# Three edits to the warm-up of a routed mixture-of-experts kernel: later weight steps, one shared tile for the first two units, and a different turn order

## The chip, the cores and the metric

The kernel runs on one core of one Trainium2 chip. The metric is the device time of one launch in microseconds (us); lower is better. The time before is 1173.4 us, the median of three runs that lie between 1171.6 and 1175.38 us.

## What is computed

The input x has 8 sequences of 2880 tokens with 192 features. Each of 8 heads (24 features) is replaced by a causal 7-tap weighted sum along the sequence. The 23040 resulting tokens then pass a two-level router (4 groups of 4 experts), and each token goes through the one expert that it picked. Cut to what matters:

```
x_unf = x_pad[:, idx, :].reshape(B, S, K, H, group)          # 7 neighbours of each token
x = einsum('hk,bskhg->bshg', softmax(weight), x_unf)         # 8 heads, K = 7
g_idx = argmax(x @ w_group); e_idx = argmax(x @ w_expert[g]) # one group, one expert in it
for each of the 16 experts (192 -> 1024 -> 192):
    out[tokens of e] = g_w * e_w * (relu(x[tokens] @ w1[e]) @ w2[e])
```

## The kernel before, in words

The work has two kinds. A **unit** is a stretch of 4, 8 or 12 blocks of 120 tokens; there are 18 of them, of 4, 8, 12, 8, 8 and 8 blocks and then twelve of 12. A unit loads its rows of x into the tile `xin` (L205, L207), runs the 7-tap sum as eight TensorE products with a band matrix (L409), one for each head, copies each into the tile `xc` on ScalarE (L418), transposes `xc` (L428, L438), forms the router's logits (L448, L451), picks group and expert on VectorE (L483 to L512), writes `xc` with the router's weight to a table of tokens in HBM, `xcd` (L514, issued on ScalarE's queue), counts positions with two small products (L523, L524), builds a list of token numbers for each expert with one-hot products (L549 to L570) and scatters it to `idtab` (L581, on GpSimd). In the text below the units are called the first to the eighteenth; in the code they are `u` = 0 to 17.

A **slot** is up to 256 tokens of one expert. It reads its token numbers (`idp`, L976), gathers the rows from `xcd` (L653), transposes them (L666, L667) and runs the two layers (L684; L702, L706). All fp32 products of a slot are built from pairs of rounded and residual parts, so an expert's weights are loaded in five transfers (L602, L603, L604, and L606 twice; 1.84 MB with the part that is loaded twice) and then **split** in four steps: a copy on ScalarE (L618, L626, L633) and a subtraction on VectorE (L619, L627, L634) each. The raw weights have three buffers of each of their two kinds (`raw` and `rawc`), and a buffer comes free when its split is done.

The slots come in three portions. The first holds one slot of each of the 16 experts and can open when the first five units have been scattered (`NEED = 5`). The second needs twelve units, the third all eighteen.

Units are Python generators. One call of `step()` in the program advances one live unit to its next `yield`. Up to three units are live in the warm-up; a new one joins when the youngest has taken a given number of steps (`SK`). Before the change the live units take turns in a circle. The warm-up loop counts its steps in `k`, and the list `KPRE` says after which step the loads of the first expert are issued, then its four splits, then the loads of the second expert and three of its splits. When the fifth unit's list has been scattered, the loop ends; the first two slots are opened, 100 more steps are taken (`AHEAD`), and the first slot is transposed. From there the steps of the remaining units are spread between the parts of the slots.

This is the order of the program. The order on each engine is laid out afterwards by a planner, which lets an instruction pass others that its own model of the time sees as not ready. A few instructions are pinned among each other (`pin`): the transfers of x up to the fifth unit, the first expert's five transfers, and ScalarE's copies of the splits. On one engine, and on one issuing queue, what stands behind a waiting instruction waits too.

The tile `xin` has two buffers; the first two units (4 and 8 blocks) share one. The tile `xc` has three, and before the change each unit takes one, so that the fourth unit has to wait until the first unit's write to `xcd` has landed, the fifth for the second's, the sixth for the third's.

Of the kernel before, what the change touches and what calls it, by code (L numbers as in the profile page):

```python
# [9 lines left out]
F32 = mybir.dt.float32  # L10
# [10 lines left out]
P = 128  # L21
BT = 120
UB = 12
# [13 lines left out]
def conv_moe_kernel(  # L37
# [50 lines left out]
    units = []  # L88
# [7 lines left out]
    NEED = 5  # L96
# [37 lines left out]
    FRH = 0  # L134
    UG = [0, 5, 6, 1, 5, 8, 0, 5, 6, 0, 5, 7, 0, 5, 6, 2, 5, 10]
    SK = [8, 8, 6, 11, 10, 9, 9]
    KPRE = [5, 6, 16, 33, 35, 47, 63, 68, 79]
    CEU = 0
    CEH = (1, 3, 5, 7)
    PF = 1  # L140
# [18 lines left out]
    pa2 = ctx.enter_context(tc.tile_pool(name="pa2", bufs=XCB))  # L159
# [13 lines left out]
    XE = XW + D2  # L173
# [72 lines left out]
    def clear_table():  # L246
        pin(PINC1, nc.sync.dma_start(
            out=bass.AP(idtab.tensor, idtab.offset, [[CAP, E], [LR, LF], [1, LR]]), in_=fill[0:LF * E, 0:LR],
        ))
        pin(PINC2, nc.sync.dma_start(  # L250
            out=idtab[DUMMY:DUMMY + SLOT, :].rearrange("(p r) c -> p (r c)", p=8), in_=fill[0:8, 0:SLOT // 8],
        ))
# [102 lines left out]
    for t in xg:  # L355
        nc.gpsimd.memset(t, 0.0)

    bands = {}

    def gaps(u):  # L360
# [3 lines left out]
    def unit(u, pre=None):  # L364
# [14 lines left out]
            if u < PFL:  # L379
                load_unit(v)  # L380
        yield
        xc = pa2.tile([P, UB, XE], F32, name="xc", bufs=3)
        split = u >= FRU
        if split:
            if "h" not in bands:
# [526 lines left out]
    credit = [0.0]  # L912
    live = []
    done = [0]
    routed = [0, 0]
    needs = {need: pi for pi, (need, _) in enumerate(portions)}

    def step():

        if routed[0] < NU and len(live) < lead[1] and (not live or max(live, key=lambda a: a[0])[1] >= (lead[0] or SK[min(routed[0], len(SK)) - 1])):  # L920
            u = routed[0]
            live.append([u, 0, unit(u, xin0 if u == 0 else None)])
            routed[0] += 1
        if not live:
            return
        done[0] += 1
        cur = live.pop(0)
        cur[1] += 1
        try:
            next(cur[2])  # L930
            live.append(cur)
        except StopIteration:
            pass
# [11 lines left out]
    def advance(rate):  # L945
        credit[0] += rate
        while credit[0] >= 1.0:
            credit[0] -= 1.0
            step()
# [84 lines left out]
    def open_slot(i):  # L1034
        if i >= len(plan):
            return
        pi, e, s = plan[i]
        if closing:
            wait[0] -= 1
            if wait[0] <= 0 or closing[0] == pi:  # L1040
                open_portion(closing.pop())
        while pi != "tail" and pi not in idps:
            step()
            if closing:
                open_portion(closing.pop())
        rate[0] = max(
            [(stages_to(portions[q][0]) - done[0]) / (max(starts[q] - MARGIN - i, 1) * 2 * NF)
             for q in starts if q not in idps] + [0.0])
        if late and (pi == "tail" or e >= 2):
            next(late[0], None)  # L1050
        if pi == "tail":
            W = tail_weights(i)
            ids = idps["tail"][:, e]
            known = N
        else:
            W = pre.pop(e if pi == 0 else None, None) or weights(e * D, e * F, PENG(pi, e)) if s == 0 else opened[i - 1][0]
            ids = idps[pi][:, e, 2 * s:2 * s + 2]
            known = sum(n for _, n in units[:portions[pi][0]]) * BT
        for q in range(i + 1, i + 1 + TAHEAD):
            if tab[0] is not None and len(units) == routed[1]:  # L1060
                tail_weights(q, False)
        opened[i] = (W, ids)
        gathered[i] = gather(ids, known, tiles(i))
# [3 lines left out]
    while routed[1] < portions[0][0]:  # L1067
        step()
        if k == KW:
            router_weights()  # L1070
        if k == 4:
            clear_table()
        for i in [i for i, kk in enumerate(KPRE) if kk == k]:
            e, q = divmod(i, 5)
            if q == 0 and e < 2:
                pre[e] = weights(e * D, e * F, {k: nc.gpsimd for k in PREG[e]})
            elif e < 2 and 4 * e + q <= KN:
                split_one(pre[e])
        k += 1
# [157 lines left out]
```

## Time and profile before

| | before |
|---|---|
| median of three runs | 1173.4 us (1171.6 to 1175.38) |
| the profiled execution | 1170.84 us, its span 1169.0 us |
| TensorE busy | 1111.7 us, 95% |
| VectorE, ScalarE, GpSimd busy | 804.5, 690.1, 498.2 us |
| mean granted TensorE clock | 0.977 |
| transfers | 195.63 MB, 167 GB/s over the span |

PE is TensorE, PEld its loading of the stationary operand, DVE VectorE, ACT ScalarE, POOL GpSimd, SP the engine that issues most transfers; a q behind a name is that engine's issuing queue. In a row of the timeline the columns are start, duration in us, engine, line, operation, output and inputs, shape and count, and in brackets how long the engine had been idle and what released it. In the view of stretches the columns are the stretch, its length, each engine's busy time with its number of instructions, the granted TensorE clock as a fraction, the DMA engines' busy share and GB/s. In the view of waits a row says who waited for whom, with the total in us, the number of times and the longest.

### The profile page before, as it was taken

To read this page: it belongs to the slowest core of one execution; us is meant where nothing else is said; L and a number is where in the kernel's file an instruction comes from. 1 tells how busy PE (TensorE), PEld (TensorE's weight loads), DVE (VectorE), ACT (ScalarE), POOL (GpSimd) and SP (SyncE) were. 2 spreads that over 40 slices of the span, in tenths; PEclk is the share of its full clock that TensorE was granted. 3 is DMA by queue.
4 is the path that set the end of the run, shared out by engine and by line. 5 is a ranking of instruction groups with operands and counts; after the bars stand their busy time and mean duration, and the time that the engine had idled before them with its cause. 6 is when DMAs were issued, how large, how long until landed. Compare 5 with 4: busy or idle time off the path is not lost.

```text
span 1169.0 us, 23803 instructions
## 1 busy us (share of the span) xinstructions
PE 1111.7 (95%) x8468; PEld 1079.3 (92%) x8468; DVE 804.5 (69%) x1668; ACT 690.1 (59%) x1374; POOL 498.2 (43%) x443
## 2 busy tenths in 40 slices
PE   5887999999999999999999999999999999999994
PEld 4766999998999999999999999999999999998984
DVE  4756788887877676666678565656565656688772
ACT  5544677657655555656554555555555656677772
POOL 2103234434434343434344444444444445578771
PEclk8879999999999999999999999999999999999997
DMA  8766699989775654546354574545454545599960
GB/s 228 217 182 178 173 213 230 226 203 268 217 194 143 165 156 118 143 116 170 95 162 95 155 203 128 142 128 141 130 141 128 140 118 167 146 243 266 248 160 19
DMA packets 167212, 195.63 MB, mean 167 GB/s; under 512 B 22500, under 2 KB 144333, under 8 KB 167086
## 3 DMA queue, kind: packets, MB, share of 16 engines
q1 hardware_dynamic: 125006, 140.41, 44.6%
q0 software_dynamic: 18752, 35.85, 10.5%
q10 hardware_dynamic: 23328, 17.80, 6.2%
q8 instruction: 67, 1.10, 0.4%
q14 instruction: 59, 0.48, 0.1%
HBM read 158.79 MB, written 36.58 MB: 167 GB/s over the span
## 4 chain that ended last, share of the span: by engine, by line
PE 79%; DVE 5%; DMA 4%; issue 3%; ACT 3%; another core or an unknown queue 0%; POOL 0%; POOLq 0%; ACTq 0%; DVEq 0%; SPq 0%
PE ph L684 33%; PE po L702 21%; PE po L706 10%; PE pm L409 3%; DMA xg<-xcd,idpt 3%; PE pm L451 2%; PE pm L666 2%; PE pm L667 2%; PE pm L428 1%; PE ph L719 1%; PE pm L448 1%; DVE hl L690 1%; DVE ohl L549 1%; DMA idtab<-lsi,rowi 1%; ACT cw L633 1%
## 5 line engine op out<-in xcount | busy, mean ns | idle before, releaser
L702 PE MATMUL po<-cw,hh 128*128 128x384 f32 x1424 | 443.4, 369 | 5.9 <-DVE ys L754 5.9
L684 PE MATMUL ph<-xa,ah 128*128 128x256 f32 x1424 | 390.2, 296 | 1.9 <-DVE xa L669 1.5
L757 POOL DMA_INDIRECT out<-ys,idp x160 | 167.8, 1049 | 447.4 <-DVE ys L754 348.8
L706 PE MATMUL po<-cw,hl 128*128 128x192 f32 x1424 | 357.3, 251 | 0.0
L690 DVE SCALAR_TENSOR_TENSOR hl<-ph,hh 128x512 fp32r<-128x512 f32 x356 | 241.2, 686 | 163.5 <-ACT hh L689 149.3
L689 ACT ACTIVATE hh<-ph 128x512 fp32r<-128x512 f32 x356 | 210.8, 594 | 205.8 <-PE ph L684 170.2
L702 PEld LDWEIGHTS po<-cw,hh 128*128 128x128 f32 x1424 | 268.6, 189 | 9.7 <-DVE ys L754 7.6
L684 PEld LDWEIGHTS ph<-xa,ah 128*128 128x128 f32 x1424 | 271.0, 190 | 5.0 <-DVE xa L669 1.6
L706 PEld LDWEIGHTS po<-cw,hl 128*128 128x128 f32 x1424 | 272.6, 191 | 1.5
L653 POOL DMA_INDIRECT xg<-xcd,idp x160 | 190.0, 1187 | 62.0 <-issue 29.6
L684 PE MATMUL ph<-xb,bh 128*128 128x256 f32 x712 | 201.9, 284 | 0.3 <-DVE xb L673 0.3
L684 PE MATMUL ph<-xb,bl 128*128 128x256 f32 x712 | 201.8, 283 | 0.0
L684 PE MATMUL ph<-xa,al 128*128 128x256 f32 x712 | 201.3, 283 | 0.0
L684 PEld LDWEIGHTS ph<-xa,al 128*128 128x128 f32 x712 | 136.5, 192 | 2.1
L684 PEld LDWEIGHTS ph<-xb,bl 128*128 128x128 f32 x712 | 136.7, 192 | 0.0
L684 PEld LDWEIGHTS ph<-xb,bh 128*128 128x128 f32 x712 | 136.2, 191 | 0.4 <-DVE xb L673 0.4
L634 DVE TENSOR_TENSOR cw<-rawc,cw 128x768 fp32r<-128x768 f32 x114 | 105.3, 953 | 18.3 <-ACT cw L633 13.7
L619 DVE TENSOR_TENSOR al<-raw,ah 128x1024 fp32r<-128x1024 f32 x57 | 70.5, 1238 | 38.8 <-ACT ah L618 21.6
L754 DVE SCALAR_TENSOR_TENSOR ys<-po,xg,ys 128x192 f32<-128x192 f32 x187 | 76.2, 416 | 23.2 <-ACT ys L753 18.1
L633 ACT ACTIVATE cw<-rawc 128x768 fp32r<-128x768 f32 x114 | 91.0, 837 | 1.8 <-DMA rawc<-in_moe_w 1.4
L672 ACT ACTIVATE xb<-pm 64x256 fp32r<-64x256 f32 x98 | 36.0, 367 | 93.4 <-DVE xa L669 86.2
L753 ACT ACTIVATE ys<-po,xg 128x192 f32<-128x192 f32 x187 | 75.8, 418 | 22.2 <-PE po L706 12.0
(216 smaller groups left out, 1561.0 us busy)
## 6 DMA issues: line engine op xcount, KB each, us to landing
rawc<-in_moe_w SPq DMA_DIRECT2D x114, 384.0 KB
raw<-in_moe_w SPq DMA_DIRECT2D x57, 512.0 KB
raw<-in_moe_w SPq DMA_DIRECT2D x114, 256.0 KB
xcd<-xc ACTq DMA_DIRECT2D x13, 1085.6 KB
xin<-in_x SPq DMA_DIRECT2D x7, 1134.0 KB
xc<-in_moe_w SPq DMA_DIRECT2D x18, 384.0 KB
xin<-in_x SPq DMA_DIRECT2D x6, 1039.5 KB
xin<-in_moe_w SPq DMA_DIRECT2D x9, 512.0 KB
```

The costliest lines, as they stand in the source:

```text
L619: eng.get(k, nc.vector).tensor_tensor(out=al, in0=ra, in1=ah.bitcast(F32), op=ALU.subtract)
L633: pin(PINW, nc.scalar.activation(out=cw[:, fs, 0, :], in_=rc[k - 2], func=AF.Copy))
L634: eng.get(k, nc.vector).tensor_tensor(out=cw[:, fs, 1, :], in0=rc[k - 2], in1=cw[:, fs, 0, :].bitcast(F32), op=ALU.subtract,)
L653: nc.gpsimd.indirect_dma_start(out=xs[:, t, :], out_offset=None, in_=xcd[0:known, :], in_offset=bass.IndirectOffsetOnAxis(ap=ids[:, t, 0:1 ...
L684: nc.tensor.matmul(out=hp[:, j], lhsT=wgt[:, fs], rhs=xx, start=i == 0, stop=i == len(ops) - 1)
L689: nc.scalar.activation(out=hh, in_=hp, func=AF.Relu)
L690: nc.vector.scalar_tensor_tensor(out=hl, in0=hp, scalar=0.0, in1=hh.bitcast(F32), op0=ALU.max, op1=ALU.subtract,)
L702: nc.tensor.matmul(out=oo[t][:, 0:2 * D], lhsT=hh[:, j, ts], rhs=cw[:, f].rearrange("p a d -> p (a d)"), start=f == 0, stop=False,)
L706: nc.tensor.matmul(out=oo[t][:, 0:D], lhsT=hl[:, j, ts], rhs=cw[:, f, 0, :], start=False, stop=f == NF - 1,)
L753: nc.scalar.activation(out=ys[:, t, :], in_=oo[t][:, D:2 * D], func=AF.Copy, scale=g)
L754: nc.vector.scalar_tensor_tensor(out=ys[:, t, :], in0=oo[t][:, 0:D], scalar=g, in1=ys[:, t, :], op0=ALU.mult, op1=ALU.add,)
L757: nc.gpsimd.indirect_dma_start(out=outviews[nscat[0] % len(outviews)], out_offset=bass.IndirectOffsetOnAxis(ap=ids[:, t, 0:1].bitcast(U32) ...
```

## The change

It has three parts. The list `KPRE` gets other step numbers: the first expert's loads go from step 5 to step 10 and its splits from 6, 16, 33 and 35 to 26, 29, 36 and 39; the second expert's loads go from 47 to 88 and three of its splits from 63, 68 and 79 to 128, 134 and 144. The second unit no longer takes an `xc` tile of its own: it uses blocks 4 to 11 of the first unit's. And `step()` no longer takes the live units strictly in a circle: once exactly one of the first five units is live beside later ones, that unit gets every second step and the others share the rest.

```
-    KPRE = [5, 6, 16, 33, 35, 47, 63, 68, 79]
+    KPRE = [10, 26, 29, 36, 39, 88, 128, 134, 144]
...
+    shared = []
...
-        xc = pa2.tile([P, UB, XE], F32, name="xc", bufs=3)
+        if u == 1:
+            xc = shared[0][:, units[0][1]:UB]
+        else:
+            xc = pa2.tile([P, UB, XE], F32, name="xc", bufs=3)
+            if u == 0:
+                shared.append(xc)
...
+    odd = [False]
...
-        cur = live.pop(0)
+        first = [a for a in live if a[0] < NEED]
+        others = [a for a in live if a[0] >= NEED]
+        cur = live[0]
+        if len(first) == 1 and others:
+            odd[0] = not odd[0]
+            cur = first[0] if odd[0] else others[0]
+        live.remove(cur)
```

## The prediction

> **What bounds the kernel now.** I read the page first (busy shares), then the stretches, then TensorE's waits, then the timeline of the first 120 us.
>
> ```profile
> span 1169.0 us, 23803 instructions
> PE 1111.7 (95%) x8468; PEld 1079.3 (92%) x8468; DVE 804.5 (69%) x1668; ACT 690.1 (59%) x1374; POOL 498.2 (43%) x443
> ```
>
> TensorE is busy 95% of the span. The change leaves its work as it is, so it can only take away, or add, time in which TensorE idles or runs at a reduced clock. The stretches say where that time is:
>
> ```profile
> 0.00:20.60 20.60, 10.74 (x56) 9.88 (x56) 9.45 (x51) 11.44 (x34) 8.38 (x32) 1.00 0.80 206
> 20.60:30.00 9.40, 6.17 (x18) 4.41 (x18) 4.56 (x14) 5.10 (x11) 0.00 (x0) 0.64 1.04 281
> 30.00:46.40 16.40, 16.40 (x141) 15.54 (x140) 11.00 (x42) 13.00 (x36) 2.09 (x1) 1.00 0.83 238
> 46.40:64.00 17.60, 8.74 (x57) 7.13 (x57) 13.53 (x54) 4.87 (x16) 1.95 (x2) 0.61 0.72 175
> 64.00:80.00 16.00, 14.88 (x79) 12.82 (x78) 7.50 (x33) 7.47 (x22) 0.97 (x1) 0.68 0.70 206
> ...
> 101.50:120.00 18.50, 11.78 (x69) 9.76 (x69) 10.04 (x41) 6.33 (x18) 6.00 (x6) 0.82 0.65 169
> ...
> 400.00:1100.00 700.00, 695.60 (x5346) 686.43 (x5345) 472.81 (x855) 413.02 (x770) 329.52 (x285) 1.00 0.55 153
> ```
>
> From 400 to 1100 us there is nothing to gain: 695.6 of 700 us are busy at full clock. In the warm-up there is. I count a stretch's loss as its idle time plus busy time times (1 - clock). From 20.6 to 30: 3.23 + 6.17 x 0.36 = 5.4 us. From 46.4 to 64: 8.86 + 8.74 x 0.39 = 12.3. From 64 to 80: 1.12 + 14.88 x 0.32 = 5.9. From 101.5 to 120: 6.72 + 11.78 x 0.18 = 8.8. From 30 to 46.4 nothing is lost. What TensorE waited for, and what ScalarE waited for behind it:
>
> ```profile
> PE ph L409 <- DVE band L339: 8.7, 1, 8.7
> PE pm L570 <- DVE ohv L557: 4.6, 4, 1.6
> PE pm L409 <- ACT lg L454: 3.5, 1, 3.5
> PE ph L570 <- DVE ohv L557: 3.4, 1, 3.4
> PE ph L409 <- DMA xin<-in_x: 3.2, 1, 3.2
> PE pm L409 <- ACT xc L418: 2.2, 1, 2.2
> ```
>
> ```profile
> ACT xc L418 <- DMA xcd<-xc: 12.0, 3, 6.0
> ACT lg L454 <- remote: 3.9, 1, 3.9
> ```
>
> The 8.7 us for the band matrix at the start is not touched.
>
> **Part one: the first expert's loads behind the third unit's x.** Counting the generators' steps in the code, the second unit's first step, which also requests the third unit's x, is step 9. The loads at step 5 stand ahead of it, at step 10 behind it; both are pinned, so the queue follows.
>
> ```profile
> 12.84 0.35 SPq L207 DMA_DIRECT2D xin<-in_x  x1
> 23.84 1.31 PE L409 MATMUL ph<-xin,band 126*120 126x288 f32 x2 [3.23 <-DMA xin<-in_x]
> 24.95 1.17 PE L409 MATMUL pm<-xin,band 126*120 126x288 f32 x2
> ...
> 86.71 0.65 PE L409 MATMUL po<-xin,band 126*120 126x288 f32 x2
> 87.20 0.65 PE L409 MATMUL pm<-xin,band 126*120 126x288 f32 x2
> ```
>
> TensorE is through with the second unit at 20.6 and waits 3.23 us for an x that was issued at 12.84 behind the expert. With the expert's 1.84 MB out of its way, x comes 1.84 MB / 281 GB/s = 6.5 us earlier, at about 17.3, before it is wanted. After the wait a pair of products takes 1.17 us, later 0.65 (and starts 0.49 apart): the clock is reduced for a while, and that goes with the wait. So up to 5.4 us. In return the first expert's data come 12 x 126 rows x 768 B = 1.16 MB, or 4.1 us, later; its copies are moved 10 to 20 steps back as well, so that they should rarely hold up ScalarE. I take a gain of 5.0; the ends are 0 (ScalarE stuck behind a late copy for as long as TensorE was behind x) and 5.4.
>
> The Trainium skill ("TensorE: Matmul & The Clock Gate", Part 1) says that the array gets half its pulses until it has been busy for some 3.4 us, so that every wait costs 1.7 us more. The trace agrees here (2.2 us of clock lost from 20.6 to 30). With this wait and two later ones gone, that rule's clock term would be 5.1 us in place of the 4.2 that I use (2.2 here, 2.0 below); the sum by it would be -12.4 in place of -11.5, an estimate.
>
> **Part two: the second expert's splits late.** Steps 63, 68 and 79 lie among the fourth unit's heads; 128, 134 and 144 lie after the fifth unit's, before its list (step 154 after the change).
>
> ```profile
> 35.73 1.23 DVE L619 TENSOR_TENSOR al<-raw,ah 128x1024 fp32r<-128x1024 f32 x1 [0.80 <-ACT ah L618]
> 39.34 1.05 ACT L626 ACTIVATE bh<-raw 128x1024 fp32r<-128x1024 f32 x1
> 40.42 1.22 DVE L627 TENSOR_TENSOR bl<-raw,bh 128x1024 fp32r<-128x1024 f32 x1 [1.39 <-ACT bh L626]
> 40.96 5.06 SPq L606 DMA_DIRECT2D rawc<-in_moe_w  x2
> 43.11 0.33 ACTq L514 DMA_DIRECT2D xcd<-xc  x1
> 51.40 0.34 ACT L418 ACTIVATE xc<-ph 120x192 f32<-120x192 f32 x1 [5.26 <-DMA xcd<-xc]
> 55.18 0.32 ACTq L514 DMA_DIRECT2D xcd<-xc  x1
> 62.58 0.33 ACT L418 ACTIVATE xc<-pm 120x192 f32<-120x192 f32 x1 [6.03 <-DMA xcd<-xc]
> ```
>
> The stall from 46.4 on is a chain. The second unit's write is issued at 43.11 and lands 8.29 us later; the fifth unit's first copy needs its buffer, so ScalarE stands still for 5.26 us; behind it stands the third unit's exponential, so the third unit's write goes out only at 55.18, and 7.4 us later the sixth unit's copy has waited 6.03. Ahead of 43.11 stand 1.23 + 1.22 us of the second expert's subtractions on VectorE and a 1.05 us copy on ScalarE. Without them I put the write 2.4 us earlier. Its landing shortens too: the loads that share the transfers then (40.96) are the third expert's, which need buffers that the second expert's splits set free. By size the third unit's landing bounds it, 7.4 x 8/12 = 4.9 us; between that and 8.29 I take 6. So 4.7 of the 5.26 us go, and of the 6.03 some 2.4.
>
> In TensorE's time: the 2.2 us wait goes, one ohv wait of 1.6 goes with VectorE's relief, 1.6 of the 3.4 and 0.6 of a last one of 1.6 go: 6.0 us. Of the 8.2 us lost to the clock from 46.4 to 80 (3.4 + 4.8) I take 2.0, less than their share. Together 8.0; the ends are 0 and 18.2.
>
> The cost is at the new place.
>
> ```profile
> 34.66 1.05 ACT L618 ACTIVATE ah<-raw 128x1024 fp32r<-128x1024 f32 x1
> 42.71 0.84 ACT L633 ACTIVATE cw<-rawc 128x768 fp32r<-128x768 f32 x1
> 44.66 0.95 DVE L634 TENSOR_TENSOR cw<-rawc,cw 128x768 fp32r<-128x768 f32 x1
> 85.15 0.97 POOL L581 DMA_INDIRECT idtab<-lsi,rowi  x1 [12.81 <-DVE lsi L578]
> 91.43 0.39 SPq L976 DMA_DIRECT2D idp<-idtab  x1
> 96.33 1.07 POOL L653 DMA_INDIRECT xg<-xcd,idp  x1 [10.21 <-DMA idp<-idtab]
> 109.50 0.27 PE L666 MATMUL pm<-ident,xg 128*128 128x128 f32 x1
> ```
>
> It is 1.05 + 1.05 + 0.84 = 2.9 us of ScalarE and 1.23 + 1.22 + 0.95 = 3.4 us of VectorE, in a stretch where each is busy 7.5 of 16 us. What queues behind them is the fifth unit's choice of expert and its write. Ends 0 and 3.4; I take 1.5, since both engines are half idle. The loads of the second expert are not pinned: the third expert's (40.96) already run some 190 steps ahead of their place, so they may stay early. That costs nothing while the raw buffers hold, and is no gain.
>
> **Part three: the shared tile.** It spares the fourth unit's wait on the first unit's write: 12.0 - 5.26 - 6.03 = 0.7 us on ScalarE, while TensorE was fully busy (30 to 46.4). The fifth unit still needs the second unit's write. I take 0; ends 0 and -0.7.
>
> **Part four: the turns.** The warm-up loop falls from 162 to 155 steps. Five of the seventh unit's heads, 5 x 0.49 = 2.4 us of TensorE, move behind the fifth unit's list. The work is moved, not removed, and 100 steps still follow before the first slot. I take 0; ends -2.4 and 2.4. The chain from list to first transpose (85.15 to 109.50, 24.35 us) stays covered by sixth to ninth unit as before; the 8.8 us lost from 101.5 on, 3.5 of them behind a ScalarE wait whose source the profile does not name, I leave, with ends of 4 us either way. The main part is replanned too, without a reason for either sign: 0, ends 2.
>
> **The sum.** -5.0 - 8.0 + 1.5 = -11.5 us. The profiled execution took 1170.84 us (span 1169.0 and 1.84 around it), so 1159.3; the median of the runs shown stands 2.56 higher, so 1161.9.
>
> **The rivals.**
> - *The waits on the writes stay* (the buffers are asked for in the same order, and the copies come earlier by as much as the writes do). Only part one is left: -5.0 + 1.5, so 1169.9. For it: the sixth unit's wait of 6.03 us follows a landing of 7.4 us that nothing shortens directly. Against: the relief on VectorE lies ahead of the writes alone.
> - *Slower: the third expert's loads fall into the opening chain.* They wait for the second expert's splits. If those run at 78 us or later, 1.84 MB (6.5 us at 281 GB/s) lies beside the fifth unit's write, the list's scatter, the read of `idp` and the first gathers, which TensorE must wait out. 6.5 + 3.4 - 5.0 = +4.9, so 1178.3. It decides from the point where the third expert's L606 issues lie between the fifth unit's write and the first gather. Against: step 128 lies among the sixth unit's first heads, one of whose copies ran at 62.58, and from 101.5 on the engines have bandwidth free (0.65). The Trainium skill ("DMA: Bandwidth & Descriptors", Queues, rings and completion order) says that an engine takes turns between the queues that have work; by that such loads would halve a write's rate, which speaks for this rival.
> - *More*: the whole chain from 46.4 to 80 dissolves: -5.0 - 18.2 + 1.5, so 1151.7. For it: each wait there causes the next, and the clock falls with them.
> - *The change does not do what it says*: the planner already reorders, and puts x or the splits where they were. 1173.4.
>
> **How the numbers follow.** The forecast gets 0.40 (1156 to 1168 by itself), the waits that stay 0.15, slower 0.20, more 0.13, nothing 0.12. 0.3% (3.5 us) is about what a measurement of this kernel can tell from no change. Faster by more: 0.40 + 0.13 + half of 0.15 = 0.61. Within: the other half and 0.09 of the 0.12, 0.16. Slower: 0.20 + 0.03 = 0.23. The range from 1149 to 1178 reaches from the far case to the slower one, with the unknown ends of the opening in it.
>
> **What would show it.** Part one: the L207 issue of the third unit ahead of the first L602 behind the table's clearing, no wait of L409 on x near 20 us, clock near 1 from 20 to 30. Part two: no second split before the fifth unit's heads, the total of ScalarE's waits on xcd down from 12.0 to some 5. Its cost: waits of VectorE's L483 chain on copies of the splits. The turns: the scatter of the fifth unit some 12 us ahead of 85.15 and the first L684 ahead of 110.9 by as much. I am wrong if the first L684 is earlier by that and the end is not, if new waits on xcd take the old ones' place, or if the stretch before the first L684 loses more than 8.8 us.

## The result and the profile after

The change makes the kernel slower: 1190.41 us (1185.01 to 1194.36) against 1172.5 us (1167.51 to 1175.38) for the kernel before on the same chip, a ratio of 1.0148 [1.0114, 1.0182]. The forecast was 1161.9 us, with 0.23 on slower; the range ended at 1178. The profiled execution of the changed kernel took 1194.36 us, its span 1192.6 us. A trace shows one execution, which need not be the typical one: this is the slowest of its six, and those of p_second and p_later below are the fastest of ten and twelve, so what an edit is worth is read from the medians and ratios. In the changed kernel every line from the second hunk of the diff on stands six lines later (L409 is L415, L418 is L424, L514 is L520, L684 is L690, and so on).

The page of the kernel after, its span and busy time:

```profile
span 1192.6 us, 23804 instructions
...
PE 1133.0 (95%) x8468; PEld 1097.2 (92%) x8468; DVE 803.8 (67%) x1668; ACT 690.0 (58%) x1374; POOL 494.9 (41%) x443
```

TensorE runs the same 8468 instructions as before. Its busy time rose from 1111.7 to 1133.0 us, its idle time within the span only from 57.3 to 59.6. So 21.3 of the 23.6 us are busy time, spent on the same instructions at a lower clock. The stretches say where (columns as before, the clock behind the engines):

```profile
20.60:30.00 9.40, 6.94 (x38) 4.72 (x37) 6.95 (x28) 8.97 (x21) 0.00 (x0) 1.00 1.00 246
30.00:46.40 16.40, 14.58 (x70) 14.22 (x70) 5.30 (x19) 6.00 (x19) 1.05 (x1) 0.57 0.63 148
46.40:64.00 17.60, 16.93 (x96) 15.81 (x94) 8.83 (x39) 7.91 (x22) 0.99 (x1) 0.63 0.53 132
64.00:80.00 16.00, 11.26 (x63) 10.64 (x63) 11.59 (x44) 5.18 (x13) 0.97 (x1) 0.57 0.78 211
...
101.50:120.00 18.50, 15.55 (x99) 14.13 (x98) 7.96 (x33) 5.93 (x18) 8.00 (x8) 0.66 0.74 209
400.00:1100.00 700.00, 696.14 (x5381) 687.95 (x5380) 470.50 (x862) 405.70 (x765) 320.50 (x282) 1.00 0.54 148
```

From 20.6 to 30 the clock is now full (0.64 before), as forecast. From 30 to 46.4, where nothing was lost before, TensorE now does 70 instructions in place of 141, at 0.57. From 400 to 1100 the two kernels are alike.

The timeline of the kernel after, with the x of the third unit, the first expert's loads and copies, TensorE's waits behind them, and the chain from list to first slot:

```profile
8.54 0.33 SPq L207 DMA_DIRECT2D xin<-in_x  x1
8.91 3.54 SPq L608 DMA_DIRECT2D raw<-in_moe_w  x1
23.44 0.65 PE L415 MATMUL pm<-xin,band 126*120 126x288 f32 x2
23.50 1.06 ACT L624 ACTIVATE ah<-raw 128x1024 fp32r<-128x1024 f32 x1
25.75 1.08 ACT L632 ACTIVATE bh<-raw 128x1024 fp32r<-128x1024 f32 x1
26.99 0.87 ACT L639 ACTIVATE cw<-rawc 128x768 fp32r<-128x768 f32 x1
28.26 0.89 ACT L639 ACTIVATE cw<-rawc 128x768 fp32r<-128x768 f32 x1
28.48 0.63 PE L434 MATMUL pm<-ident,xc 120*128 120x120 f32 x4 [1.66 <-ACT xc L424]
31.82 0.25 PE L576 MATMUL po<-ohv,ohl 120*128 120x32 f16 x4 [1.87 <-DVE ohv L563]
...
94.65 0.97 POOL L587 DMA_INDIRECT idtab<-lsi,rowi  x1 [11.55 <-DVE lsi L584]
96.93 0.39 SPq L989 DMA_DIRECT2D idp<-idtab  x1
123.97 0.42 PE L672 MATMUL pm<-ident,xg 128*128 128x128 f32 x1
125.38 0.50 PE L690 MATMUL ph<-xa,ah 128*128 128x256 f32 x1
```

Part one's x comes as forecast (8.54, 12.84 before) and the third unit's heads run at 0.65 us a pair. But the first expert's four copies now lie on these heads: ScalarE is busy 8.97 of 9.4 us, and TensorE runs dry at 28.48 and 31.82. The fifth unit's scatter comes 9.5 us later than before, not 12 earlier; the first slot's first transposition 14.5 us later.

The waits of ScalarE up to 130 us:

```profile
ACT tb L445 <- remote: 3.7, 1, 3.7
ACT xc L424 <- DMA xcd<-xc: 2.7, 2, 1.6
```

The waits on the writes fell from 12.0 to 2.7 us, more than the 5 forecast. The gain that was hung on them is not in the time.

### The profile page after: what moved, and what is told of

Same layout as the page of the kernel before. It is cut to its first block, busy times and chain, and to the rows that moved or that the text cites. A ratio compares the mean times of both kernels' runs of the same rounds, so it can differ in the third digit from the quotient of the medians.

```text
span 1192.6 us, 23804 instructions
## 1 busy us (share of the span) xinstructions
PE 1133.0 (95%) x8468; PEld 1097.2 (92%) x8468; DVE 803.8 (67%) x1668; ACT 690.0 (58%) x1374; POOL 494.9 (41%) x443
## 4 chain that ended last, share of the span: by engine, by line
PE 77%; DMA 8%; DVE 7%; issue 3%; ACT 3%; SPq 1%; another core or an unknown queue 0%; ACTq 0%; POOLq 0%; POOL 0%; DVEq 0%
PE ph L690 31%; PE po L708 19%; PE po L712 9%; PE pm L415 4%; DMA xg<-xcd,idpt 4%; PE pm L457 2%; PE pm L672 1%; PE pm L434 1%; PE pm L673 1%; DVE hl L696 1%; PE pm L454 1%; DMA idtab<-lsi,rowi 1%; PE po L457 1%; PE ph L415 1%; DMA rawc<-in_moe_w 1%
## 5 line engine op out<-in xcount | busy, mean ns | idle before, releaser
L690 PE MATMUL ph<-xa,ah 128*128 128x256 f32 x1424 | 391.4, 297 | 2.8 <-DVE xa L675 2.4
L690 PEld LDWEIGHTS ph<-xa,ah 128*128 128x128 f32 x1424 | 272.0, 191 | 6.1 <-DVE xa L675 2.6
L659 POOL DMA_INDIRECT xg<-xcd,idp x160 | 187.3, 1170 | 55.0 <-issue 31.4
L690 PE MATMUL ph<-xb,bh 128*128 128x256 f32 x712 | 202.3, 284 | 0.2 <-DVE xb L679 0.2
L690 PE MATMUL ph<-xb,bl 128*128 128x256 f32 x712 | 202.2, 284 | 0.0
L690 PE MATMUL ph<-xa,al 128*128 128x256 f32 x712 | 201.9, 284 | 0.0
L690 PEld LDWEIGHTS ph<-xa,al 128*128 128x128 f32 x712 | 137.1, 193 | 2.2
L690 PEld LDWEIGHTS ph<-xb,bl 128*128 128x128 f32 x712 | 137.2, 193 | 0.0
L690 PEld LDWEIGHTS ph<-xb,bh 128*128 128x128 f32 x712 | 136.7, 192 | 0.3 <-DVE xb L679 0.3
```

Of the source, the lines that this page charges most:

```text
L659: nc.gpsimd.indirect_dma_start(out=xs[:, t, :], out_offset=None, in_=xcd[0:known, :], in_offset=bass.IndirectOffsetOnAxis(ap=ids[:, t, 0:1 ...
L690: nc.tensor.matmul(out=hp[:, j], lhsT=wgt[:, fs], rhs=xx, start=i == 0, stop=i == len(ops) - 1)
```

## The experiments

Every ratio is against the kernel before, run in turn with it on the same chip. To see whether a difference is clock or idle time, I split each run's span in two: the **lost clock**, span x (1 - mean granted clock), and the **rest**. Both are given as the difference of the means to those of before on the same chip (us); their standard error is 1 to 1.5 us, 2 to 3 where marked *. The split is over all of the span, idle time too, so it is a rough measure. For the whole change the clocks of before are those of its profiled run and of the other sets (lost clock 26.4 to 27.1, rest 1143.8 to 1145.9).

| kernel | median us | ratio [95%] | lost clock | rest |
|---|---|---|---|---|
| the whole change | 1190.41 | 1.0148 [1.0114, 1.0182] | +12.5 | +4.4 |
| a_first: first expert's steps alone | 1180.56 | 1.0054 [1.0000, 1.0108] | +8.0* | -2.1 |
| a_second: second expert's steps alone | 1178.68 | 1.0054 [1.0024, 1.0084] | +5.8 | -0.9 |
| a_tile: shared tile alone | 1176.96 | 1.0021 [0.9999, 1.0043] | +1.7 | +1.1 |
| a_turns: turns alone | 1185.65 | 1.0084 [1.0055, 1.0114] | +5.7 | +4.7 |
| c_noturn: the change without turns | 1176.35 | 1.0033 [1.0000, 1.0066] | +6.4 | -2.1 |
| c_later: the change, first splits at 60 to 78 | 1183.84 | 1.0105 [1.0073, 1.0138] | +10.6* | +2.6 |
| d_later: c_noturn, first splits at 60 to 78 | 1180.99 | 1.0094 [1.0058, 1.0129] | +10.5* | -0.9 |
| k_after: the change and 16 extra products once | 1191.61 | 1.0173 [1.0127, 1.0219] | +12.0 | +7.6 |
| f_after: the change and fill products | 1188.62 | 1.0174 [1.0109, 1.0239] | +1.0* | +18.0 |
| t_ahead: a_turns, seven more steps | 1175.02 | 1.0032 [1.0007, 1.0056] | +3.6 | +0.2 |
| t_after: the change, seven more steps | 1169.34 | 1.0028 [0.9999, 1.0056] | +4.1 | -0.1 |
| r4_second: a_second, four raw buffers | 1176.10 | 1.0030 [1.0009, 1.0052] | +4.9 | -1.2 |
| r4_before: before, four raw buffers | 1173.11 | 1.0011 [0.9987, 1.0034] | -0.4 | +1.5 |
| p_second: a_second, loads held | 1162.98 | 0.9972 [0.9954, 0.9991] | -1.9 | -1.4 |
| p_before: before, loads held | 1163.10 | 0.9971 [0.9950, 0.9992] | -2.5 | -0.6 |
| p_after: t_after, loads held | 1168.09 | 1.0008 [0.9983, 1.0034] | +1.6 | -0.9 |
| p_noturn: c_noturn, loads held | 1173.19 | 1.0012 [0.9979, 1.0045] | +1.8 | -0.8 |
| p_later: d_later, loads held | 1173.56 | 1.0001 [0.9973, 1.0028] | +3.3 | -4.5 |

(p_after's split leaves out one run, whose clock record of 0.925 stands against 0.973 to 0.981 in the others.)

### Each part alone

a_first and a_second each take one half of the new list, a_tile the second hunk's shared tile, a_turns the new `step()`:

```
a_first:   KPRE = [10, 26, 29, 36, 39, 47, 63, 68, 79]
a_second:  KPRE = [5, 6, 16, 33, 35, 88, 128, 134, 144]
```

> The old kernel with only the first expert's five step numbers changed (10, 26, 29, 36, 39). Theory (clock): its copies (4 us of ScalarE) and subtractions (4.3 us of VectorE) now fall on the third unit's heads, TensorE runs dry at 27 to 32 us for some 3.8 us, the clock drops to half and stays there through the routers' small products: at least 10 us of reduced clock between 30 and 60 us, and the time 8 to 16 us above the old kernel. Rival (opening): the cost comes from the second expert's late splits; then this run is 0 to 6 us faster than the old kernel, because the third unit's x is early.

> The old kernel with only the second expert's four step numbers changed (88, 128, 134, 144). Theory (clock): the wait on x at 20 us stays as before and the clock recovers at 30 us as before, so the time is within 5 us of the old kernel's. Rival (opening): the late splits hold up the fifth unit and put the third expert's loads beside the first gathers; 8 to 17 us slower, the first L684 some 10 us later than 110.9.

> The old kernel with only the shared tile. Theory (clock): the order is nearly that of the old kernel, so within 4 us of it. Rival (tile): sharing makes the fifth unit wait for two writes and the later units for other buffers; 5 us or more slower.

> The old kernel with only the new turns. Theory (clock): nothing changes before the sixth unit comes in, at about 50 us, so the first 46 us are the same, and the time is within 4 us. Rival (turns): less work of the sixth and seventh unit stands ahead of the fifth unit's list, TensorE runs dry behind it; 5 us or more slower.

No part gains. The tile is close to nothing, as forecast. Both halves of the list cost 0.5%, all of it clock (for the first half the interval reaches down to nothing). The turns are the dearest part, as their rival said, and the only one whose rest rises clearly. a_first stays below the 8 to 16 us of its theory. a_second lies between its two, but its first slot product comes where the rival put it, at 119.77 (110.89 before). The parts alone add up to 2.1%, the whole is 1.5%; with these intervals that is no clear difference.

**a_first** shows part one by itself. In the timeline of this kernel TensorE's two waits behind the copies are:

```profile
27.03 0.63 PE L428 MATMUL pm<-ident,xc 120*128 120x120 f32 x4 [1.67 <-ACT xc L418]
...
30.36 0.26 PE L570 MATMUL po<-ohv,ohl 120*128 120x32 f16 x4 [2.32 <-DVE ohv L557]
```

and the stretch behind them loses its clock, which was full there before (the view of stretches):

```profile
30.00:40.00 10.00, 9.64 (x46) 9.45 (x46) 3.77 (x16) 3.68 (x11) 1.06 (x1) 0.52 0.63 186
```

Measured as busy time x clock from the start, this kernel is 2.4 us of work ahead of the kernel before at 30 us (17.1 against 14.7) and 2.6 us behind at 40 (22.1 against 24.7).

### Without the turns, and the first splits elsewhere

c_noturn leaves the turns out of the whole change. c_later (with the turns) and d_later (without) move the first expert's splits away from the third unit's heads:

```
c_later, d_later:  KPRE = [10, 60, 66, 72, 78, 88, 128, 134, 144]
```

> The changed kernel without the new turns (step list and shared tile stay). By the runs of single parts the turns cost 0.84%, so if parts add up this is 9 to 10 us faster than the changed kernel, at about 1180. Theory (clock): the stretch at half clock from 32 to 58 us stays (it lies ahead of the turns), the one at 108 to 125 us goes or shrinks. Rival: the parts do not add up, because the clock's long dip comes from the step list; then within 4 us of the changed kernel.

> The changed kernel with the first expert's splits moved on to steps 60, 66, 72 and 78, clear of the third unit's heads; the third unit's x stays early. Theory (clock): ScalarE and VectorE are free at 23 to 31 us, TensorE does not run dry there, the clock stays at full through the routers of the second to fourth unit, and the time falls by 6 to 14 us against the changed kernel. Rival: the splits cost the same wherever they are; within 3 us of the changed kernel.

> The change without its turns, and the first expert's splits at steps 60, 66, 72 and 78 in place of 26 to 39. If the two corrections add up: the change without turns is at 1176.35, and the later splits brought 6.6 us on the whole change (1183.84 to 1190.41), so 1170 us, 0.997 of before. If the later splits help only because the fifth unit's turns have moved the list, it stays at 1175 to 1178. If they run on the fifth unit's copies without the turns too, it is 1179 to 1183.

The turns cost 1.1% on top of the rest (1.0148 to 1.0033). Where the first splits go does not settle it: without the turns later is worse (1.0094 against 1.0033), with them it looks better (1.0105 against 1.0148), but there the intervals overlap. d_later shows how part one's gain is lost again. Its stretches, and that of before for the first of them:

```profile
20.00:40.00 20.00, 18.39 (x145) 16.42 (x144) 10.96 (x47) 16.07 (x43) 1.06 (x1) 1.00 0.86 232
40.00:60.00 20.00, 12.03 (x72) 10.11 (x70) 16.18 (x61) 5.42 (x17) 0.99 (x1) 0.61 0.63 175
80.00:140.00 60.00, 50.32 (x335) 44.50 (x334) 35.22 (x118) 25.80 (x67) 11.05 (x11) 0.80 0.68 170
```

```profile
20.00:40.00 20.00, 16.58 (x101) 13.94 (x102) 11.06 (x38) 13.27 (x34) 2.09 (x1) 0.83 0.93 265
```

Busy time x clock is 18.39 x 1.00 = 18.4 us here and 16.58 x 0.83 = 13.8 before: with x early and no split on the heads TensorE is 4.6 us ahead at 40 us, very nearly the 5.0 of the prediction. In the timeline of d_later ScalarE then stands at the next thing:

```profile
37.02 0.33 ACTq L520 DMA_DIRECT2D xcd<-xc  x1
46.89 0.33 ACT L424 ACTIVATE xc<-ph 120x192 f32<-120x192 f32 x1 [5.25 <-DMA xcd<-xc]
```

A write issued 6 us earlier than before (37.02, not 43.11) and landing in 9.9 us brings the next copy only 4.5 us forward (46.89, not 51.40), with the same 5.25 us wait, and TensorE idles 8 of the next 20 us. That takes about half of the lead: 2 us are left at 60 us and also at 80 (busy time x clock, counted as above). The rest, and 6 us more, goes from 80 to 140 us: 50.32 x 0.80 = 40.3 us of work there against 49.0 before (52.15 x 0.94, shown below). The second expert's late splits are in this kernel too, and a_second alone does 39.2 us in that stretch.

### Is the clock itself the bound?

k_after runs the second pair of products of the fourth unit eight times more (16 extra dense products); f_after puts one 128x480 product ahead of each of the router's small ones up to the ninth unit. Both add work whose result is overwritten.

```
k_after, ahead of a head's products:
+            for _ in range(8 if u == 3 and h == 1 else 0):
+                nc.tensor.matmul(out=ps[0:BT, 0:nb * HC], lhsT=band[0:R, h, :], rhs=xin[0:R, :, cs], start=True, stop=True)
f_after, ahead of the router's products:
+            for _ in range(1 if u <= 8 else 0):
+                nc.tensor.matmul(out=lgp[0:P, 0:QN], lhsT=ident, rhs=ta[:, 0:QN], start=True, stop=True)
```

> The changed kernel with eight extra copies of one of the fourth unit's head products ahead of the real one, at the point (34 us) where the clock has just dropped: pure extra work of TensorE, 5.1 us at half clock or 2.6 at full, overwritten by the real product. Theory (clock): a few us of dense streaming bring the clock back, so the stretch to 58 us runs at full clock; the loss by clock falls by some 8 us and the time by 3 to 8 us against the changed kernel, in spite of the added work. Rival (order): the clock only follows the waits and the order of the work; the clock stays at half and the time rises by 3 to 5 us.

> The changed kernel with one extra dense product (128 x 480 fp32, 0.4 us at full clock) ahead of each router call of the first nine units, 18 calls, 7.3 us of TensorE work at full clock, overwritten by the real products. Theory (clock): the routers' small products no longer keep the clock down; the loss by clock (39 us in the changed kernel) falls below 28 us and the time stays or falls by up to 8 us although 7.3 us of work are added. Rival (order): the time rises by 7 us or more and the loss by clock stays.

In the timeline of k_after the clock is full again behind the extra products:

```profile
32.51 4.76 PE L415 MATMUL pm<-xin,band 126*120 126x192 f32 x16
...
37.57 0.57 PE L460 MATMUL pm<-wr,ta 128*120 128x20 f32 x4
```

But over all its runs the lost clock is what it was (+12.0, +12.5 without the products), and the rest rises by 3.2 us, about what the 16 products take at full clock (2.6). The expected gain is not there, and the run does not say what a clock regained for good would be worth.

f_after does not say it either. The fill is larger than the text above counts: TensorE runs 42 more products than in the kernel after (8468), from 18 to 147 us.

```profile
PE 1128.3 (95%) x8510; PEld 1086.3 (92%) x8510; DVE 805.4 (68%) x1668; ACT 689.5 (58%) x1374; POOL 494.7 (42%) x443
```

At full clock they start 0.40 us apart, so they are some 17 us of added work, not 7.3. The lost clock falls by 11.5 us, the rest rises by 13.6, less than the work that was added, and the time is the same within the intervals. So the clock gave back no more than the fill took. Whether TensorE would run into other waits without it, or finish sooner, is not shown, and with that it stays open whether the clock bounds the warm-up.

### The turns: seven steps

The loop ends after 155 steps instead of 162, and 100 more steps follow either way. t_ahead and t_after give these seven back, on the turns alone and on the whole change:

```
-    AHEAD = 100
+    AHEAD = 107
```

> Before with the turns alone, and AHEAD 107 in place of 100, so that the first slot is transposed after step 262 again, as before the change (the turns alone: step 255, 1185.65 us, 1.0084). Theory one, the seven missing unit steps: the sixth to eighth units are seven steps behind when the slots begin, their copies on ScalarE then meet the slots' work, and TensorE runs dry at 140 to 200 us (3.6 us with the turns alone, none before) and once more at 280 to 360. Then TensorE's idle time from 140 to 200 is under 1 us here, and the median is 1172 to 1178 us. Theory two, the order itself: with the fifth unit's small products taken every second step there are fewer heads beside them, the clock falls from 100 to 120 us, and nothing of that comes back with more steps: the median is 1182 to 1188 us, the stretch from 80 to 140 loses 14 to 17 us as with the turns alone (10 before).

> The whole change with AHEAD 107 in place of 100. If the seven missing steps cost the same here as with the turns alone (1185.65 to 1175.02, 10.6 us), 1178 to 1181 us. If here the fifth unit's chain and the half clock from 32 to 58 us bound the time, it stays at 1186 to 1191, and the idle time of 160 to 200 us (3.1 us) alone goes.

The median of t_ahead lies where theory one put it; t_after came out lower than either of its ranges (beside it the kernel before took 1166.59 us). The stretch from 140 to 200 us, in the kernel before, with the turns alone, with the turns and seven steps, after the change, and after it with seven steps:

```profile
140.00:200.00 60.00, 60.00 (x479) 57.82 (x478) 51.20 (x123) 41.01 (x90) 21.12 (x18) 1.00 0.90 217
```

```profile
140.00:200.00 60.00, 56.46 (x445) 53.48 (x445) 46.89 (x102) 37.95 (x82) 23.52 (x18) 1.00 0.78 202
```

```profile
140.00:200.00 60.00, 60.00 (x479) 57.86 (x479) 50.29 (x114) 40.88 (x87) 21.63 (x19) 1.00 0.92 221
```

```profile
140.00:200.00 60.00, 56.90 (x448) 53.79 (x446) 46.55 (x103) 36.19 (x81) 16.35 (x15) 1.00 0.72 185
```

```profile
140.00:200.00 60.00, 60.00 (x477) 57.80 (x476) 50.46 (x119) 40.35 (x87) 21.30 (x18) 1.00 0.88 220
```

TensorE idles 3.5 and 3.1 us there without the seven steps and not at all with them. The timeline of a_turns shows one such wait: a later unit's copy stands behind the issue of a write that waits for VectorE, and TensorE behind the copy.

```profile
153.25 0.42 ACT L418 ACTIVATE xc<-pm 120x288 f32<-120x288 f32 x1 [2.90 <-DVE xc L512]
153.72 0.75 PE L409 MATMUL pm<-xin,band 126*120 126x288 f32 x2 [0.97 <-ACT xc L418]
```

On both pairs the rest falls by 4.5 us (+4.7 to +0.2, +4.4 to -0.1). That much of the turns' cost is shown: later units' steps that came seven too late. Such a stall is not made up here, where slots run between the units' steps.

The clock's share is not settled. It falls by 2.1 us on the one pair and by 8.4 on the other, although TensorE, VectorE and ScalarE do the same work in the same order in both kernels of a pair until the first slot, and the queues until the first gathers. In the profiled executions the whole change and t_after differ long before the seven steps can act. Counted by the starts of TensorE's products, t_after is 17.5 us ahead when the orders part (after 526 products) and 25.1 at the last one; t_ahead is 0.8 us ahead of a_turns there and 11.0 at the last one. So behind that point, where seven steps can act, these executions gain 7.6 and 10.2 us, and the 17.5 us have another cause. TensorE in the kernel after:

```profile
39.59 0.85 PE L415 MATMUL ph<-xin,band 126*120 126x192 f32 x2
...
40.63 0.85 PE L415 MATMUL po<-xin,band 126*120 126x192 f32 x2
```

and the same two products in t_after:

```profile
37.87 0.85 PE L415 MATMUL ph<-xin,band 126*120 126x192 f32 x2
...
38.91 0.53 PE L415 MATMUL po<-xin,band 126*120 126x192 f32 x2
```

The clock came back at 39.0 in t_after and only at 59.6 in the kernel after. The traces show a grid behind that: in all twenty the granted clock is either 1.0 or 0.5, and each of the 236 stretches of either that end within a trace is a whole multiple of 3.41 us, from one to ten of them at 0.5. Here it was three (10.2 us) in t_after and eight (27.3 us) in the kernel after. Why three or eight, whether by the chip, the moment, or arrival times a few tenths apart, stays open: each was run beside the kernel before, but they were not run beside each other.

### Late splits, late loads

With the second expert's splits late, the third expert's loads come late. Two ways to test that: four raw buffers, so that those loads need not wait for the late splits, with the kernel before as a control; and the loads of the third and fourth expert, and the read of the first list, pinned on SP's queue so that these loads come behind that read.

```
r4_second, r4_before:
-  wraw.tile([P, F], F32, name="raw")
+  wraw.tile([P, F], F32, name="raw", bufs=4)
p_second, p_before, p_after, p_noturn, p_later:
-    PINI = False
+    PINI = True
-        hold = tc.keep_in_program_order if NPIN[0] < npin[0] <= NPIN[1] else lambda ins: ins
+        hold = tc.keep_in_program_order if npin[0] in (1, 3, 4) else lambda ins: ins
```

In r4_second, r4_before, p_second and p_before the order on TensorE, VectorE, ScalarE and GpSimd is exactly that of the kernel they are made from; only SP's queue differs.

> Only the second expert's steps late (1178.68 us, 1.0054), and four raw buffers in place of three, so that the third expert's first two kinds of loads need only the first expert's splits and no longer the second's late ones. Theory one, the loads: with three buffers the third expert's L602 to L604 were issued at 69 to 76 us, and the write at 78.66 landed 9.2 us later, with ScalarE standing still for 6.99 us. Here these loads are issued ahead of 55 us, ScalarE's wait on that write is under 3 us, the first slot product comes at 111 to 115 us (119.8 with three), and the median is 1170 to 1175. Theory two, the splits' own time on ScalarE and VectorE beside the fifth unit: the first slot product stays at 118 to 121 us and the median at 1177 to 1181.

> Before with four raw buffers, the control of the run with four. In the kernel before, the third expert's first loads come at 40 to 62 us already, so theory one (late loads are what costs) gives no difference: 1170 to 1176 us. If loads cost wherever they meet a unit's write, those that come earlier here (20 to 45 us) lengthen the writes of the second and third unit (waits on them 12.0 us in all), and the median is 1176 to 1182.

r4_second was no clean test: the fourth expert's loads took the third's place (issued at 68.94 to 72.92), and ScalarE still waited 5.20 us on the write. r4_before is a warning: in its trace ScalarE waits 18.9 us on writes in place of 12.0, and over its runs the time is that of before (1.0011), though this execution is the slowest of its ten. The whole change has 2.7 us of such waits and is slower. So the sum of ScalarE's waits on writes does not give the time. The hold is the cleaner test. First a_second (its L602 at 75.42 is already the fourth expert's; L604, the third's, was issued at 74.54), the timeline of SP and ScalarE and the stretch from 80 to 140:

```profile
69.46 0.47 SPq L603 DMA_DIRECT2D raw<-in_moe_w  x1
75.42 0.62 SPq L602 DMA_DIRECT2D raw<-in_moe_w  x1
78.66 0.32 ACTq L514 DMA_DIRECT2D xcd<-xc  x1
87.88 0.41 ACT L418 ACTIVATE xc<-ph 120x288 f32<-120x288 f32 x1 [6.99 <-DMA xcd<-xc]
```

```profile
80.00:140.00 60.00, 49.00 (x327) 42.68 (x326) 34.76 (x118) 25.64 (x67) 11.03 (x11) 0.80 0.67 171
```

> Only the second expert's steps late (1178.68 us, 1.0054), and the third and fourth expert's loads held behind the read of the first list (L976, some 90 us) on SP's queue; the order on TensorE, VectorE, ScalarE and GpSimd is the same as without that. Theory one, loads beside a unit's write: the write at 78.7 lands in under 6 us (9.2 before this edit), ScalarE's wait of 6.99 us on it falls under 3.5, the stretch from 80 to 140 loses under 16 us (20.5 before this edit), and the median is 1170 to 1175. Theory two, the splits' own time: the waits change little and the median is 1177 to 1181. A third case: the loads then lie beside the gathers at 92 to 110 us; then the first transposition comes later than 119 us and the median is 1180 or more.

> The same edit of SP's queue alone on the kernel before, where the third and fourth expert's loads (40.4 to 46.1 and 62.0 us) lie beside the third and fourth unit's writes (landing in 8.3 and 7.4 us). If loads lengthen the writes, these land in under 6 us, ScalarE's waits on them fall from 12.0 us to 7 or less, and the median is 1165 to 1169 us, 0.994 to 0.997 of before: this is the second effect that the prediction's part two counted on. If the writes take as long without them, 1170 to 1174. If the loads cost more beside the gathers at 92 to 110 us than they did beside the writes, 1175 to 1180.

p_second, the same rows:

```profile
78.56 0.32 ACTq L514 DMA_DIRECT2D xcd<-xc  x1
83.96 0.42 ACT L418 ACTIVATE xc<-ph 120x288 f32<-120x288 f32 x1 [2.62 <-DMA xcd<-xc]
93.39 0.78 SPq L602 DMA_DIRECT2D raw<-in_moe_w  x1
```

```profile
80.00:140.00 60.00, 56.13 (x441) 50.64 (x441) 45.91 (x146) 34.89 (x85) 17.94 (x16) 0.97 0.86 234
```

The fifth unit's write, issued at the same time, lands in 5.4 us in place of 9.2, ScalarE waits 2.62 in place of 6.99, and the stretch loses 5.6 us (3.87 idle, 56.13 x 0.03) in place of 20.8 (11.00 idle, 49.00 x 0.20). The time goes from 1.0054 to 0.9972, faster than the kernel before. The late splits themselves cost nothing that shows; the loads did. Nor do the late splits gain anything that shows: with the loads held, it is 0.9972 with them and 0.9971 without (p_before).

In p_before the second unit's write (timeline of ScalarE; the expectation calls the second and third unit's writes the third and fourth's), and the stretch from 80 to 140, with that of before last:

```profile
44.13 0.33 ACTq L514 DMA_DIRECT2D xcd<-xc  x1
49.42 0.33 ACT L418 ACTIVATE xc<-ph 120x192 f32<-120x192 f32 x1 [2.26 <-DMA xcd<-xc]
```

```profile
80.00:140.00 60.00, 55.92 (x439) 50.41 (x439) 45.43 (x146) 34.60 (x83) 18.03 (x16) 0.97 0.87 231
```

```profile
80.00:140.00 60.00, 52.15 (x407) 46.83 (x407) 41.00 (x138) 31.54 (x78) 15.78 (x16) 0.94 0.62 165
```

It lands in 5.3 us (8.29 before), and the time is 0.9971. This is the second effect that part two counted on, a write that lands sooner without the third expert's loads beside it. The change could not bring it, since it moved the loads from one write to another: in the kernel after, loads are issued at 79.06, 82.52 and 83.41, the fifth unit's write goes out at 87.17, and the copy behind it comes 8.0 us later. There ScalarE waits only 1.57 us for it, so what these loads cost within the whole change is not shown by that wait.

> The whole change with AHEAD 107, and with the third and fourth expert's loads held behind the read of the first list. If the missing steps and the loads beside the fifth unit's write account for the loss together, it is within 0.4% of before, 1168 to 1176 us. If what is left is the first expert's splits on the third unit's heads and the clock that they cost (9.8 us lost at 40 to 60), 1177 to 1183. If neither correction holds on the whole change, 1185 or more.

> The change without its turns, and the third and fourth expert's loads held behind the read of the first list. Without the hold it was 1.0033, and the hold was worth 0.8% on the second expert's steps alone (1.0054 to 0.9972). If the first expert's steps cost what they did alone (0.54%), 1.000 to 1.003 of before. If their cost too was the loads beside the fifth unit's write, 0.993 to 0.997.

> The same with the first expert's splits at steps 60, 66, 72 and 78 in place of 26 to 39 (1.0094 without the hold). Without the hold TensorE had done 4.8 us more work at full clock by 40 us than before the change, had lost it again by 100 us, and the stretch from 80 to 140 lost some 20 us. If the loads took that gain, 0.990 to 0.995 of before. If splits at 60 to 80 us hold up the fourth and fifth unit by themselves, 0.999 to 1.006.

With seven steps and held loads the whole change is where the kernel before is (1.0008 [0.9983, 1.0034]); most of that is the steps, since the hold's part (from 1.0028) is within the intervals. Held loads lower the lost clock in all five pairs (by 7.7, 2.5, 2.5, 4.6 and 7.2 us in the order second, before, after, noturn, later); in time the gain is clear of the intervals for second, before and later only. p_noturn and p_later gain nothing over p_second: with the first expert's new steps and the shared tile they come out 0.3 to 0.4% higher, at the edge of what the intervals can tell, wherever the splits lie. p_second and p_before beat both kernels, by 0.3% of before.

## Why the prediction was wrong

The time is 28.5 us above the forecast, and three terms of the sum carry that. Alone, part one measured +0.5% where -0.4% was forecast, part two +0.5% in place of -0.6%, and part four +0.8% in place of nothing.

**Part one** (-5.0). Its first sentence held: x early, no wait at 20 us, full clock to 30. The step that failed is the clause that the first expert's copies "should rarely hold up ScalarE". They came right on the heads, and a_first shows the price: +8.0 us of clock, +0.5% [0.0, 1.1] in place of a gain of 5.0 us. The lower end of 0 was no bound, since a copy that holds up the heads starts a new wait and a loss of clock behind it. And d_later shows that the 5.0 itself, where it is had (4.6 us at 40 us), does not last: the next wait on a write takes about half, and the stretch from 80 to 140 us, behind the late loads (73.26 to 74.78 in d_later), takes more than the rest.

**Part two** (-8.0, +1.5). In the whole change ScalarE's waits on writes fell as forecast. In a_second, part two by itself, the two old ones fell too (from 5.26 and 6.03 to 0.99 and 2.55), but a new one of 6.99 took their place, which the prediction had named as a sign of being wrong. Wrong were two steps. The 8.0 us counted a write that goes out earlier without the splits and lands sooner without the loads. With the loads held either way the late splits bring nothing (0.9972 and 0.9971), so only the landing is real, and it belongs to the loads, which the change moved and did not take away. And "that costs nothing while the raw buffers hold": they did not hold, the third expert's L603 and L604 and the fourth's L602 came at 69 to 76 us, and the write beside them landed 4 us later. That is the mechanism of the rival on the slower side, which got 0.20; its place was the fifth unit's write ahead of the list, not the gathers, and its price on part two alone 0.8%, some 10 us (a_second against p_second), where the rival had 6.5 + 3.4. On the whole change that price is not clear of the intervals (1.0028 to 1.0008).

**Part three** (0): 1.0021 [0.9999, 1.0043], right within the measurement.

**Part four** (0, ends 2.4): the mis-sized term. It measured some 10 us alone (1.0084; the medians are 12.2 apart) and 1.1% on the whole change (1.0148 against 1.0033). "The work is moved, not removed" overlooked that behind the first slot the later units' copies have no slack on ScalarE either: seven steps that come later cost 4.5 us of rest, and TensorE's idle time from 140 to 200 us (3.5 and 3.1 us) is part of it. What the turns cost in clock ahead of the first slot has no shown cause. The list's scatter, forecast 12 us ahead of 85.15, came at 84.70 in a_turns and 94.65 in the whole change. Taking the fifth unit's steps more often did not make it faster; that its chain of VectorE, ScalarE and writes is the limit fits this, but no run tests it alone.

**The clock.** The prediction let the clock come back soon after a wait. It stayed at half for 27.3 us (32.2 to 59.6) in the kernel after. The Trainium skill ("TensorE: Matmul & The Clock Gate", Part 1) has it come back after some 3.4 us of being busy; the trace does not agree, at least not with busy as the profile counts it. From 32 to 56 us of the kernel after (the view of stretches) TensorE is busy all the time and the clock is half:

```profile
32.00:56.00 24.00, 24.00 (x118) 23.59 (x116) 6.11 (x28) 8.21 (x24) 1.05 (x1) 0.51 0.71 172
```

Nor did every wait cost the same: behind the wait of 3.23 us before, 2.2 us went to the clock, behind those of 1.66 and 1.87 us after some 13.7 (half of 27.3).

## What to carry to other kernels

When a load is pushed back, look which small transfer it lands beside: here 0.8 MB of weights (262 kB of the third expert's, 524 kB of the fourth's) beside one unit's write cost more than anything the moved work saved, and holding these loads back on their queue, and nothing else, was worth 0.8% there (0.3% on the kernel before, 0.2 to 0.9% over five kernels, the 0.2% not clear of the intervals). Before counting a removed wait as a gain, name the next wait on the same chain and how far away it is. And an order of turns that ends a warm-up loop sooner also ends it with less work done; compare at an equal number of steps.

## What the runs showed of the hardware

The granted clock is 1.0 or 0.5 and holds for whole multiples of 3.41 us, in all twenty traces. With TensorE busy without a gap, the half clock lasted about 10 us in one execution (t_after, 28.7 to 39.0) and 27 us in another of the same instruction order. In a third it lasted 6.8 us and ended at 36.4, during 16 extra dense products (32.51 to 37.27); since it ended in t_after without them, that they ended it is not shown. Ahead of its first record, at 15 to 20 us, the view prints a clock of 1.00 that no record backs: a pair of 192-column products took 0.85 us at 17.64 in the kernel after and 0.49 at 20.35, so TensorE ran at half there.

Over the 67 runs of before, the whole change and the four parts alone, a run's span follows its lost clock with a slope of 1.00 (correlation 0.87). Part of that is the difference between the kernels: with each kernel's own mean taken out the slope is 0.81 (0.82), and within the five sets of before the correlation is 0.57 to 0.77. So the granted clock is a large part of what differs from run to run of one program, but not all of it.

A unit's write landed in 9.2 us with weight loads beside it and in 5.4 without (a_second, p_second), another in 8.3 and 5.3 (before, p_before). ScalarE's waits of 1.9 to 4.7 us at 102 to 112 us, whose source the profile gives as "remote", are there before and after the change and in p_noturn, and absent in p_second, p_before and p_after, but also in t_after, c_later, k_after and f_after, where no loads were held; what they are stays open.
